# A pooled-attention and mixture-of-experts kernel: values summed by one operation, the first two hidden chunks joined, and a wait on output moved to the next job

## The chip, the core and the metric

The kernel runs on one core of a Trainium2 chip. A core has five engines that run their own instruction streams and meet only at semaphores: TensorE (PE in the profile, with its weight loads as PEld), VectorE (DVE), ScalarE (ACT), GpSimd (POOL) and SyncE (SP, which issues DMAs). The metric is the device time of one execution in microseconds (us), lower is better. Before the change the median of three runs is 604.17 us (603.97 to 604.62).

## The reference, cut to what matters

Attention over 8 batches, 8 heads and 576 positions, with keys and values averaged over groups of 8 neighbours (576 rows become 72), then a mixture of 8 experts of which each token takes one.

```python
k_p = k.reshape(B, H, Sp, pool, D).mean(axis=3)        # pool = 8, Sp = 72, D = 64
v_p = v.reshape(B, H, Sp, pool, D).mean(axis=3)
attn = softmax(scale * q @ k_p.T)                      # 576 x 72
x = (attn @ v_p), heads side by side                   # 4608 tokens x 512
e_idx = argmax(x @ w_gate); gate_w = its softmax share
eom = sigmoid(x @ w_output_gate)
h = relu(x[mask] @ w1[e]);  ye = h @ w2[e]             # 512 -> 1024 -> 512
out[mask] = gate_w * eom * ye
```

## The kernel before, in words

**Attention and routing** (the first 150 us) work on 36 tiles of 128 tokens, each in two halves of heads (a = 0, 1). Per half PE makes scores (L275) into `p_h`, DVE takes the row maximum `m` (L281), ACT the exponentials (L287), PE transposes them (`ptr`, L299), ACT copies them to SBUF, PE multiplies them with the pooled values `vbd` into `p_y` (L309), and DVE takes reciprocals (L326) and writes the normalised rows `xg` (L332). There are two `p_y` banks, one for each half, so the next tile's L309 of a half waits for this tile's L332 of that half.

For each of the batches 1 to 7 the values arrive by DMA in `vt` (a view of the buffer `rows`): 5 chunks of 128 partitions x 512 numbers, which are 8 neighbours x 64. GpSimd adds the upper 256 to the lower 256 of each chunk (`halve_v`, L223: chunks 0 to 2 as part 0, chunks 3 and 4 as part 1). DVE then adds 128 to 128 (in `rows`) and 64 to 64 (into `vp`), for each part, by `pool_v` (L227). GpSimd also sums the keys (`kq`, L201), which ACT scales into `kbd` (L206), and issues the scatters of finished rows to the experts' lists (L440), one for each tile.

The order on each engine is the order of the Python calls. `plan` fixes most steps to a half tile; small DVE steps (the pooling of values, `pooled`, and the routing of four tiles, `route`) stand in a queue, from which `work` takes two units after the row maximum, one after the values' matmuls and one after the normalisation. Each `yield` of `pooled` or `route` ends a unit. `pooled` is put at the queue's head.

**The tail** (152 to 175 us) is written as the string `TAIL`: the first expert's first layer for the first 384 tokens, in eight chunks of 128 hidden units. `M` is the 12 matmuls of a chunk (L659, into one of three `p_h` banks or `p_y1`), `H` the relu on ACT (L516), `L` its low part on DVE (L520), `a`/`d` and `A`/`D` the high and low halves of weights (L468, L472), `W` units of the queue (the routing of the last tiles, and the job table), `R` the first rows' places, `T` each engine's load of the table, `Y` three matmuls of the second layer (L665). Then all engines meet at a barrier (L1393).

**The experts** (175 us on) run jobs of three or two slots of 128 tokens. PE does the first layer (L1015) and the second (L996), DVE scales the result into one of three buffers (L1186), and GpSimd scatters it to `out` (L1328). GpSimd's job is `body` in the block from L1260 on: it waits for the earlier outputs, copies weights and row numbers (L1321, L1322), gathers the ids two jobs ahead (L1305), scatters its slots, and waits until all of its scatters have landed. The kernel ends at a second barrier (L1361).

Of the kernel before, what the change touches and what calls it, by code (L numbers as in the profile page):

```python
# [16 lines left out]
ALU = mybir.AluOpType  # L17
AX = mybir.AxisListType
PSUM = bass.MemoryType.PSUM

B, H, S, D = 8, 8, 576, 64
KEYS, POOL = 72, 8
N, DM, FF, E = B * S, H * D, 1024, 8
P = 128
NT = N // P
WIDE = 3
# [4 lines left out]
R = 56  # L31
# [26 lines left out]

TAIL = 'M W9 a H L W3 d M a H L W6 d M a H L W6 d M a H L W6 d A M H L W12 A D M H L A D R M H L A D T M D Y Y Y Y Y H L'.split()
F0 = TAIL.count('Y')

AHEAD = {3: 8, 2: 8, 1: 2}
# [26 lines left out]
def attention_and_routing(ctx, tc, sh, qT, kT, v, wg, wst, xs):  # L91
    nc = tc.nc
# [11 lines left out]
    vt = sh.rows[:, 0:5 * DM].rearrange("p (c f) -> p c f", c=5)  # L104
# [113 lines left out]
    def part_v(a):  # L218
        return slice(3 * a, 3 + 2 * a)
# [5 lines left out]
    def pool_v(b, a, n):  # L225
        to = vt[:, part_v(a), 0:n] if n > D else pooled_rows(b)[:, part_v(a)]
        nc.vector.tensor_tensor(to, vt[:, part_v(a), 0:n], vt[:, part_v(a), n:2 * n], op=ALU.add)  # L227

    def first_v(a):
        for n in (4 * D, 2 * D, D):  # L230
            pool_v(0, a, n)

    def place_v(b, c):
        t = vbd[b % 2]
# [250 lines left out]
    halves = list(range(AHEAD_OF_X, 8))  # L485
    layered, high, low, outputs, split_piece, split_done = [], [], [], [], [], [3, 2, 1, 0]

    def first_layer(kind):
        if kind == "M":
            f = len(layered)  # L490
            layered.append((sh.p_h + sh.p_y[1:])[f % 4][:, 0:WIDE * P])
            hidden_chunk(nc, sh, f, layered[f], f == 0)
        elif kind == "Y":
            outputs.append(output_chunk(nc, sh, len(outputs), sh.p_y[0], 0))
        elif kind == "a":
            split_hi(halves[0])
        elif kind == "d":
            split_lo(halves.pop(0))
        elif kind == "A":
            split_piece.append(len(split_piece))  # L500
            split_hi(2 * 4 + split_piece[-1], 1)
        elif kind == "D":
            split_lo(2 * 4 + split_done.pop(), 1)
        elif kind == "T":
            assert not queue
            for eng in (nc.tensor, nc.scalar, nc.vector, nc.gpsimd, nc.sync):
                sh.loaded[eng.engine] = nc.values_load_multi_w_load_instructions(
                    sh.table[0:1, 0:E + 2], [eng.engine], min_val=0, max_val=1023,
                    skip_runtime_bounds_check_because="counts of a few bits each")[1]
        elif kind == "R":  # L510
            slot_rows(lambda ins: None, nc.vector, sh, past_rows(sh, 0, 2 * WIDE), line_rows(sh, 0, 2 * WIDE), sh.number[:, 0:2 * WIDE],
                      sh.base[:, :, 0:2 * WIDE], sh.ids[:, 0:2 * WIDE], sh.at[:, 0:2 * WIDE])
        elif kind == "H":
            f = len(high)
            high.append(f)
            nc.scalar.activation(sh.ht[:, 0, f], layered[f], AF.Relu)  # L516
        else:
            f = len(low)
            low.append(f)
            nc.vector.scalar_tensor_tensor(sh.ht[:, 1, f], layered[f], 0.0, sh.ht[:, 0, f].bitcast(F32),  # L520
                                           op0=ALU.max, op1=ALU.subtract)
# [5 lines left out]

    def pooled(b):
        for a in range(2):
            for n in (2 * D, D):  # L530
                pool_v(b, a, n)
                yield 0

    tick = [0]

# [14 lines left out]
    for b in range(1, B):  # L550
        f = S * b // P + 0.5 * (b % 2)
# [77 lines left out]
    for step in sorted(x for x in plan if x > NT + 2):  # L629
        for f, args in plan[step]:  # L630
            f(*args)
    for step in TAIL:
        if step[0] == "W":
# [16 lines left out]
    return x.rearrange("p g f -> p (g f)"), x.rearrange("p g (d t) -> p d g t", d=4), halves  # L650


def hidden_chunk(nc, sh, f, acc, late):
    terms = [(d, part, x) for d in range(4) for part, x in ((0, 0), (0, 1), (1, 0))]
    if late:
        terms.sort(key=lambda term: term[2])
    for d, part, x in terms:
        o = DM * f + P * d
        i = nc.tensor.matmul(acc, sh.w1[0][:, part, o:o + P], sh.xt[:, x, d, :], start=((d, part, x) == terms[0]), stop=((d, part, x) == terms[-1]))  # L659
    return i  # L660


def output_chunk(nc, sh, f, acc, k):
# [64 lines left out]
def experts(st, nc, sh, wst, xs, out):  # L728
# [9 lines left out]
    yb = [y_all[:, DM * k:DM * k + DM] for k in range(WIDE)]  # L738
# [11 lines left out]
    q = {k: st.enter_context(nc.semaphore("m_" + k)) for k in names}  # L750
# [535 lines left out]
    @blk.gpsimd  # L1286
    def _(eng):
        copy = nc.gpsimd.tensor_copy

        def columns(u):  # L1290
            u = nc.s_assert_within(u, 0, R - WIDE, skip_runtime_bounds_check_because="there are at most 50 slots")
            return ids[:, bass.ds(u, WIDE)]

        def past(name, val):
            val = eng.to_reg(val)
            eng.wait_ge(q["on"], 1)
            eng.wait_ge(q[name], val)

        def take(u):
            copy(nx, xm[:, :, ID - DM:ID - DM + 2]).then_inc(q["c"], 1)  # L1300
            copy(src, columns(u)).then_inc(q["c"], 1)  # L1301

        def gather(sems):
            for k in range(WIDE):
                nc.gpsimd.indirect_dma_start(out=xm[:, k].bitcast(I32), out_offset=None, in_=xs,  # L1305
                                             in_offset=bass.IndirectOffsetOnAxis(ap=src[:, k:k + 1], axis=0)).then_inc(sems[k], 16)

        def ahead(u, job, more):
            if not isinstance(job, int):
                for k in range(WIDE):  # L1310
                    past(f"x{k}", 16 * job - 16)
            with eng.If(more > 0):
                take(u + 3)
            with eng.If(more <= 0):
                take(u + 2)
            past("c", 3 * job + 1)
            gather(X)

        def body(e, size, job, u, single, nth, more, last, late):
            past("y", u + 1)  # L1320
            copy(sc[:, 0:3:4 - size], nx[:, 0:size, 1]).then_inc(q["sc"], 1)  # L1321
            copy(dst, nx[:, :, 0]).then_inc(q["c"], 1)  # L1322
            past("sc", job + 1)
            past("c", 3 * job + 5)
            ahead(u + size, job + 2, more)
            for k in range(size):
                past("y", u + k + 2)
                nc.gpsimd.indirect_dma_start(out=out, out_offset=bass.IndirectOffsetOnAxis(ap=dst[:, k:k + 1], axis=0),  # L1328
                                             in_=yb[2 if k == size - 1 else k], in_offset=None, bounds_check=N - 1, oob_is_err=False).then_inc(q["out"], 16)
            past("out", 16 * (u + size))  # L1330

        eng.nop().then_inc(q["on"], 1)
        rows = table(eng)
        with eng.If(rows[E + 1] > 2):
            eng.nop().then_inc(q["c"], 2)
        with eng.If(rows[E + 1] <= 2):
            copy(src, columns(0)).then_inc(q["c"], 2)
            past("c", 2)
            gather([q["g"]] * WIDE)
            past("g", 16 * WIDE)  # L1340
        ahead(0, 1, rows[E + 1] & 1)
        eng.wait_ge(q["t"], ROWS)
        job, slot = loops(eng, rows, body)
        for k in range(WIDE):
            past(f"x{k}", 16 * job + 16)


def program():
# [54 lines left out]
def layout(q, k, v, moe_w_gate, moe_w_output_gate, moe_w1, moe_w2):  # L1403
    c = np.ascontiguousarray
    gates = np.concatenate([moe_w_gate, moe_w_output_gate], axis=1).reshape(H, D, GATE)
    wg = np.zeros((2, D, 11, GATE), np.float32)
    for a, slot, head in ((0, 0, 0), (0, 1, 1), (1, 2, 3), (1, 3, 4), (0, 4, 1), (0, 5, 2), (1, 6, 6), (1, 7, 7), (0, 8, 4), (0, 9, 5), (0, 10, 6)):
        wg[a, :, slot] = gates[head]
    rows = v.reshape(B, H, KEYS, POOL * D)
    vs = np.zeros((B, P, 5, POOL * D), np.float32)  # L1410
    for chunk, r0, head, k0, n in VROWS:
        vs[:, r0:r0 + n, chunk] = rows[:, head, k0:k0 + n]
    return {
        "qT": c(q.reshape(B, 4, 2, S, D).transpose(0, 2, 4, 1, 3)).reshape(B, P, 4 * S),
        "kT": c(k.reshape(B, 4, 2, KEYS, POOL, D).transpose(0, 2, 5, 1, 4, 3)).reshape(B, P, 4 * POOL * KEYS),
        "v": vs.reshape(B, P, 5 * POOL * D),
        "wg": wg.reshape(P, 11 * GATE),
        "wst": c(np.concatenate([
            moe_w1.reshape(E, H, D, FF).transpose(0, 2, 1, 3).reshape(E, 4, 4, 32, FF).transpose(0, 1, 3, 2, 4).reshape(E, P, 4, 8, P).transpose(0, 1, 3, 2, 4).reshape(E, P, 4096),
            moe_w2.reshape(E, 8, P, DM).transpose(0, 2, 1, 3).reshape(E, P, 4096)], axis=2)),  # L1420
    }
# [6 lines left out]
```

## Time and profile before

| | |
|---|---|
| median of three runs | 604.17 us |
| the profiled execution | 603.94 us, of which the span that the profile covers is 602.1 us |
| PE busy | 572.3 us (95%) |
| DVE, ACT, POOL busy | 365.1, 257.8, 223.1 us |
| TensorE's granted clock | full speed in every slice |

Times in the rows count from the start of the span. Where an operation of DVE overlaps the next one by some hundredths, this is its pipeline: a start-to-start distance is then what it costs. "Idle before" is put down to the event that came last.

### The profile page before, as it was taken

What the parts mean: (1) busy time and instruction counts of PE and PEld (TensorE: products, weight loads), DVE (VectorE), ACT (ScalarE), POOL (GpSimd) and SP (SyncE); (2) the same over time, 40 slices, a digit from 0 to 9 for tenths busy, and PEclk for the clock granted to TensorE, in tenths of its full rate; (3) what the DMA queues carried; (4) which work ended last, traced back from release to release, by engine and by line L of the source; (5) the groups of instructions that cost most, each with busy time, mean ns of one, the idle gap of its engine ahead of it and who ended that gap; (6) DMA issues with size and microseconds to landing.
All of it is one profiled execution on the core that took longest, in us unless ns stands there. A gap on an engine that the chain in (4) does not pass through costs nothing.

```text
span 602.1 us, 11826 instructions
## 1 busy us (share of the span) xinstructions
PE 572.3 (95%) x3427; PEld 519.2 (86%) x3428; DVE 365.1 (61%) x892; ACT 257.8 (43%) x709; POOL 223.1 (37%) x331
## 2 busy tenths in 40 slices
PE   2999999999899999999999999999999999999996
PEld 2898898888888989898989898898988898989894
DVE  6789999988888625698575323664263842232323
ACT  2988998787435304266344120441141420302120
POOL 2858789642524322233234131231202421213131
PEclk9999999999999999999999999999999999999999
DMA  9856899966377433589666213463033212010111
GB/s 337 312 236 270 316 349 369 348 232 198 140 238 182 170 99 118 147 234 335 177 215 201 62 37 88 139 195 65 35 139 102 46 21 84 2 52 19 41 30 36
DMA packets 44684, 96.61 MB, mean 160 GB/s; under 512 B 5515, under 2 KB 28475, under 8 KB 41664
## 3 DMA queue, kind: packets, MB, share of 16 engines
q1 hardware_dynamic: 29328, 48.95, 25.3%
q10 hardware_dynamic: 7488, 27.27, 13.5%
q0 software_dynamic: 7792, 19.61, 9.3%
q14 instruction: 57, 0.47, 0.3%
q8 instruction: 19, 0.31, 0.2%
HBM read 76.36 MB, written 22.91 MB: 165 GB/s over the span
## 4 chain that ended last, share of the span: by engine, by line
PE 68%; issue 2%; DVEq 0%; DVE 0%; POOL 0%; POOLq 0%
PE p_h L1015 34%; PE p_y L996 33%; PE p_y L665 1%; POOL out L1328 0%; DVE rows L1186 0%; DVEq L1189 0%; PE p_y L1050 0%; DVE q_even L1212 0%; DVEq L779 0%; DVEq L780 0%; DVEq L1219 0%; DVEq L910 0%; DVEq L837 0%; DVEq L1211 0%; DVEq L860 0%
## 5 line engine op out<-in xcount | busy, mean ns | idle before, releaser
L1095 ACT ACTIVATE ht<-p_h 128x384 fp32r<-128x384 f32 (+1 forms) x104 | 46.9, 451 | 245.9 <-PE p_h L1015 243.7
L1015 PE MATMUL p_h<-xt,w1b 128*128 128x384 f32 (+1 forms) x736 | 115.5, 317 | 1.9 <-issue 1.3
L1015 PEld LDWEIGHTS p_h<-xt,w1b 128*128 128x128 f32 x736 | 114.4, 189 | 3.2 <-issue 2.8
L1328 POOL DMA_INDIRECT out<-rows,dst x41 | 43.1, 1051 | 199.8 <-DVE rows L1186 196.6
L1197 DVE SCALAR_TENSOR_TENSOR ht<-p_h,ht 128x384 fp32r<-128x384 f32 (+1 forms) x104 | 52.3, 504 | 98.4 <-ACT ht L1095 98.3
L996 PE MATMUL p_y<-w2b,ht 128*128 128x512 f32 x480 | 110.4, 390 | 0.0
L996 PEld LDWEIGHTS p_y<-w2b,ht 128*128 128x128 f32 x480 | 89.8, 188 | 18.4
L1015 PE MATMUL p_h<-xt,w1a 128*128 128x256 f32 (+1 forms) x640 | 93.7, 306 | 1.2 <-DVE q_even L1212 1.0
L1015 PEld LDWEIGHTS p_h<-xt,w1a 128*128 128x128 f32 x640 | 92.8, 190 | 2.3 <-DVE q_even L1212 1.2
L996 PE MATMUL p_y<-w2a,ht 128*128 128x512 f32 x408 | 94.2, 390 | 0.4 <-PE p_y L665 0.4
L996 PEld LDWEIGHTS p_y<-w2a,ht 128*128 128x128 f32 x408 | 76.2, 188 | 16.4 <-issue 0.9
L1186 DVE TENSOR_SCALAR rows<-p_y,sc 128x512 f32<-128x512 f32 x41 | 30.1, 741 | 85.9 <-PE p_y L996 71.5
L287 ACT ACTIVATE p<-p_h,m 128x72 f32<-128x72 f32 x288 | 69.9, 345 | 13.4 <-DVE m L281 13.0
L309 PE MATMUL p_y<-vbd,pT 128*128 128x162 f32 (+3 forms) x400 | 68.5, 320 | 3.8 <-DVE xg L332 2.6
L1305 POOL DMA_INDIRECT rows<-xs,src x51 | 56.0, 1099 | 24.9 <-POOL src L1301 13.4
L309 PEld LDWEIGHTS p_y<-vbd,pT 128*128 128x128 f32 (+1 forms) x400 | 54.2, 179 | 8.7 <-issue 2.5
L440 POOL DMA_INDIRECT xs<-xg,where x36 | 36.1, 1003 | 42.5 <-DVE grec L326 20.7
L201 POOL TENSOR_TENSOR kq<-kq 128x288 f32<-128x288 f32 (+1 forms) x63 | 40.8, 673 | 15.0 <-DMA kq<-kT 14.2
L275 PE MATMUL p_h<-kbd,q_even 128*128 128x144 f32 (+1 forms) x160 | 28.9, 308 | 11.6 <-DMA q_even<-qT 8.8
L332 DVE TENSOR_TENSOR xg<-p_y,grec 128x240 f32<-128x240 f32 x72 | 35.3, 490 | 1.3
L1150 DVE STREAM_TRANSPOSE turned<-rows 128x512 f32<-128x512 f32 x51 | 32.4, 686 | 4.0 <-DMA rows<-xs 2.2
L275 PEld LDWEIGHTS p_h<-kbd,q_even 128*128 128x128 f32 (+1 forms) x160 | 22.9, 191 | 13.7 <-issue 9.3
(170 smaller groups left out, 660.3 us busy)
## 6 DMA issues: line engine op xcount, KB each, us to landing
stage<-wst ACTq DMA_DIRECT2D x52, 512.0 KB, 4.7
rows<-v SPq DMA_DIRECT2D x8, 1280.0 KB, 6.3
kq<-kT SPq DMA_DIRECT2D x7, 1152.0 KB, 12.0
rows<-xs SPq DMA_DIRECT2D x36, 192.0 KB, 3.8
stage<-wst SPq DMA_DIRECT2D x12, 512.0 KB, 6.0
kq<-qT SPq DMA_DIRECT2D x4, 1152.0 KB, 9.5
q_even<-qT SPq DMA_DIRECT2D x3, 1152.0 KB, 8.8
rows<-xs SPq DMA_DIRECT2D x20, 128.0 KB
```

The lines of the kernel that those rows point to most:

```text
L201: eng.tensor_tensor(k[:, :, 0:w], k[:, :, 0:w], k[:, :, w:2 * w], op=ALU.add)
L275: nc.tensor.matmul(s[r0:r0 + n, 144 * c:144 * c + 144], q_t[b][:, 2 * a + c, s0:s0 + n], kbd[b % 2][:, 2 * a + c, :], start=True, stop=True)
L287: nc.scalar.activation(pt[i % 3][:, o:o + KEYS], sv[:, h], AF.Exp, bias=m[:, h:h + 1])
L309: nc.tensor.matmul(av[r0:r0 + n, COLS * h:COLS * (h + n_heads)], pT[:, c, r0:r0 + n], vbd[b % 2][:, slot:slot + n_heads].rearrange("p h f ...
L332: nc.vector.tensor_tensor(xg[g][:, j, 0:LEAD + DM].rearrange("p (f h) -> p f h", h=H)[:, :, hs], avv[:, :, 0:GATE + D].rearrange("p h f -> ...
L440: ins = nc.gpsimd.indirect_dma_start(out=whole_rows(xs), out_offset=bass.IndirectOffsetOnAxis(ap=where, axis=0), in_=x.bitcast(I32), in_of ...
L996: i = mm(to, ht[:, h, f, P * k:P * k + P], w[:, part, o:o + DM], start=(f == 0 and part == 0 and h == 0), stop=(f == 7 and h == 1))
L1015: i = mm(to, w[:, part, o:o + P], x, start=(d == 0 and k == 0), stop=(d == 3 and k == len(terms) - 1))
L1095: act(ht[:, 0, f, 0:size * P], p_h[f % DEEP][:, 0:size * P], AF.Relu).then_inc(q["hh"], 1)
L1197: nc.vector.scalar_tensor_tensor(ht[:, 1, f, 0:n], src, 0.0, ht[:, 0, f, 0:n].bitcast(F32), op0=ALU.max, op1=ALU.subtract).then_inc(q["hl" ...
L1305: nc.gpsimd.indirect_dma_start(out=xm[:, k].bitcast(I32), out_offset=None, in_=xs, in_offset=bass.IndirectOffsetOnAxis(ap=src[:, k:k + 1], ...
L1328: nc.gpsimd.indirect_dma_start(out=out, out_offset=bass.IndirectOffsetOnAxis(ap=dst[:, k:k + 1], axis=0), in_=yb[2 if k == size - 1 else k ...
```

## The change

It has three parts.

1. For batches 1 to 7 the two DVE additions of a part become one `tensor_reduce` over four neighbours (`sum_v`). The host lays the values of these batches out so that the four neighbours that are left after GpSimd's addition are adjacent. `pooled` has two units instead of four, so the units of `route` behind it move up.
2. `TAIL` loses its last `M`, and the first `M` makes chunks 0 and 1 together (`hidden_chunks`): first all products with the high part of the tokens, of both chunks, then those with the low part. PE is one chunk further ahead in the rest of the tail.
3. GpSimd's wait for its scatters stands at the start of the next job instead of the end of this one, and after the last job behind the waits for the gathers. The bound of the scatters is kept in a register (`limit`).

```diff
-TAIL = 'M W9 a H L W3 d M a H L W6 d M a H L W6 d M a H L W6 d A M H L W12 A D M H L A D R M H L A D T M D Y Y Y Y Y H L'.split()
+TAIL = 'M W9 a H L W3 d M a H L W6 d M a H L W6 d M a H L W6 d M A H L W12 A D M H L A D R M H L A D T D Y Y Y Y Y H L'.split()
...
+    def sum_v(b, a):
+        nc.vector.tensor_reduce(pooled_rows(b)[:, part_v(a)],
+                                vt[:, part_v(a), 0:POOL // 2 * D].rearrange("p c (d r) -> p c d r", d=D), axis=AX.X, op=ALU.add)
...
         if kind == "M":
-            f = len(layered)
-            layered.append((sh.p_h + sh.p_y[1:])[f % 4][:, 0:WIDE * P])
-            hidden_chunk(nc, sh, f, layered[f], f == 0)
+            accs = {}
+            for _ in range(1 if layered else 2):
+                f = len(layered)
+                accs[f] = (sh.p_h + sh.p_y[1:])[f % 4][:, 0:WIDE * P]
+                layered.append(accs[f])
+            hidden_chunks(nc, sh, accs)
...
     def pooled(b):
         for a in range(2):
-            for n in (2 * D, D):
-                pool_v(b, a, n)
-                yield 0
+            sum_v(b, a)
+            yield 0
...
-def hidden_chunk(nc, sh, f, acc, late):
-    terms = [(d, part, x) for d in range(4) for part, x in ((0, 0), (0, 1), (1, 0))]
-    if late:
-        terms.sort(key=lambda term: term[2])
...
+def hidden_chunks(nc, sh, accs):
+    terms = [(f, d, part, x) for f in accs for d in range(4) for part, x in ((0, 0), (0, 1), (1, 0))]
+    if 0 in accs:
+        terms.sort(key=lambda term: term[3])
...
         def body(e, size, job, u, single, nth, more, last, late):
+            with eng.If(job > 0):
+                past("out", 16 * u)
             past("y", u + 1)
...
-                                             in_=yb[2 if k == size - 1 else k], in_offset=None, bounds_check=N - 1, oob_is_err=False).then_inc(q["out"], 16)
-            past("out", 16 * (u + size))
-
+                                             in_=yb[2 if k == size - 1 else k], in_offset=None, bounds_check=limit, oob_is_err=False).then_inc(q["out"], 16)
+
+        limit = eng.to_reg(N - 1)
...
         for k in range(WIDE):
             past(f"x{k}", 16 * job + 16)
+        past("out", 16 * slot)
...
+    halves = vs[1:].reshape(B - 1, P, 5, 2, POOL // 2, D).transpose(0, 1, 2, 3, 5, 4)
+    vs[1:] = halves.reshape(vs[1:].shape)
```

On DVE, around batch 3's values, these rows stood before (`rows` and `vp` are the values, `m` the row maxima, `grec` and `xg` the normalisation, `gden` and `pos` the routing of tiles 4 to 7):

```order
L281 TENSOR_REDUCE m_1_800<-p_h 128x4
L227 TENSOR_TENSOR rows<-rows 128x3x128
L227 TENSOR_TENSOR vp_803<-rows 128x192
L326 RECIPROCAL grec_721<-p_y 128x5
L227 TENSOR_TENSOR rows<-rows 128x2x128
L332 TENSOR_TENSOR xg_719<-p_y,grec_721 128x80x5
L227 TENSOR_TENSOR vp_803<-rows 128x128
L281 TENSOR_REDUCE m_0_825<-p_h 128x4
L378 TENSOR_REDUCE gden_833<-ex_715 128x4
L382 TENSOR_TENSOR pos_836<-rk_827,running 128x32
```

and these stand now:

```order
L285 TENSOR_REDUCE m_1_796<-p_h 128x4
L234 TENSOR_REDUCE vp_798<-rows 128x192
L234 TENSOR_REDUCE vp_798<-rows 128x128
L330 RECIPROCAL grec_717<-p_y 128x5
L382 TENSOR_REDUCE gden_811<-ex_711 128x4
L336 TENSOR_TENSOR xg_715<-p_y,grec_717 128x80x5
L386 TENSOR_TENSOR pos_819<-rk_805,running 128x32
```

Both sums of values now stand ahead of the reciprocal and of `xg`, where one pair and one half of the other pair stood; routing steps have moved up into the freed places. In the other six batches the sums stand in the same way, with no routing step between the reciprocal and `xg` (in batch 4 two short ones).

On PE, where the tail begins, these rows stood before (L659 are the hidden chunks, L372 and L374 the last tiles' ranks, L665 the second layer; the weight loads between the ranks are left out):

```order
L659 MATMUL p_h<-xt,w1a 128x384 x12
...
L374 MATMUL rk_2312<-oh_2301,ones 128x8
L659 MATMUL p_h<-xt,w1a 128x384 x24
L659 MATMUL p_y<-xt,w1a 128x384 x12
L659 MATMUL p_h<-xt,w1a 128x384 x36
L507 TENSOR_LOAD table
L659 MATMUL p_y<-xt,w1a 128x384 x12
L665 MATMUL p_y<-w2a,ht 128x512 x15
L1393 UNCONDITIONAL_BRANCH
```

and these stand now:

```order
L666 MATMUL p_h<-xt,w1a 128x384 x24
...
L378 MATMUL rk_2310<-oh_2299,ones 128x8
L666 MATMUL p_h<-xt,w1a 128x384 x12
L666 MATMUL p_y<-xt,w1a 128x384 x12
L666 MATMUL p_h<-xt,w1a 128x384 x36
L666 MATMUL p_y<-xt,w1a 128x384 x12
L514 TENSOR_LOAD table
L672 MATMUL p_y<-w2a,ht 128x512 x15
L1403 UNCONDITIONAL_BRANCH
```

Twelve matmuls have moved ahead of the ranks, and the last chunk ahead of the table's load. The orders of ACT and of SP are the same in both kernels.

On GpSimd, at the end of the last job and of the kernel, these rows stood before (L1295 and L780 are arithmetic on registers; waits have no row, and the one for `out` stood between L1295 and L780):

```order
L1328 DMA out<-rows,dst 4608x512
L1295 REGISTER_ALU
L780 REGISTER_ALU
L780 COMPARE_AND_BRANCH
L779 UNCONDITIONAL_BRANCH
L1295 ISA x2
L1361 UNCONDITIONAL_BRANCH
```

and these stand now, with the wait for `out` behind the last register operation:

```order
L1337 DMA out<-rows,dst 4608x512
L787 REGISTER_ALU
L787 COMPARE_AND_BRANCH
L786 UNCONDITIONAL_BRANCH
L1302 ISA x7
L1371 UNCONDITIONAL_BRANCH
```

The loop's end and the register operations stood behind the wait and stand ahead of it; five register operations are new.

## Rows read from the trace of the kernel before

**Rows 1.** Busy time by stretch: PE, PEld, DVE, ACT, POOL, then PEclk, DMA share, GB/s.
```profile
50.00:80.00 30.00, 28.92 (x229) 26.44 (x230) 27.35 (x101) 25.71 (x105) 24.12 (x34) 1.00 0.72 273
152.00:175.00 23.00, 20.85 (x116) 19.24 (x115) 20.27 (x77) 10.14 (x18) 8.23 (x8) 1.00 0.53 186
250.00:602.00 352.00, 344.59 (x1899) 313.88 (x1897) 170.49 (x264) 102.94 (x178) 91.08 (x124) 1.00 0.34 103
```

**Rows 2.** PE's timeline: start us, us, instruction, [idle before, and what ended it].
```profile
26.33 1.20 PE L309 MATMUL p_y<-vbd,pT 128*128 128x162 f32 x6 [0.47 <-DVE xg L332]
...
58.96 1.23 PE L309 MATMUL p_y<-vbd,pT 128*128 128x162 f32 x6 [0.73 <-DVE xg L332]
...
91.91 1.20 PE L309 MATMUL p_y<-vbd,pT 128*128 128x162 f32 x6 [0.30 <-DVE xg L332]
...
127.28 1.20 PE L309 MATMUL p_y<-vbd,pT 128*128 128x162 f32 x6 [0.27 <-DVE xg L332]
...
154.08 0.97 PE L659 MATMUL p_h<-xt,w1a 128*128 128x384 f32 x4 [0.61 <-DVE xt L483]
...
155.82 0.19 PE L372 MATMUL rk<-oh,tri 128*128 128x40 bf16 x1 [0.77 <-DVE oh L363]
...
175.23 0.94 PE L665 MATMUL p_y<-w2a,ht 128*128 128x512 f32 x3 [0.99 <-PEq L1393]
```

**Rows 3.** The chain that ended last, its last step: start us, us, what.
```profile
598.09 1.00 POOL out L1328
```

**Rows 4.** Groups of DVE instructions by shape, 20 to 130 us: busy, mean ns, idle.
```profile
L227 DVE TENSOR_TENSOR rows<-rows 128x384 f32<-128x384 f32 x7 | 6.8, 976 | 1.7 <-POOL rows L223 1.7
L227 DVE TENSOR_TENSOR vp<-rows 128x192 f32<-128x192 f32 x7 | 3.8, 544 | 0.2
L227 DVE TENSOR_TENSOR rows<-rows 128x256 f32<-128x256 f32 x7 | 3.2, 464 | 0.0
L227 DVE TENSOR_TENSOR vp<-rows 128x128 f32<-128x128 f32 x7 | 2.1, 297 | 0.0
```

**Rows 5.** Two lines with sums on DVE: duration ns min/median/max, first and last start, forms.
```profile
L348 DVE TENSOR_REDUCE lg<-xg x9: 671/676/678, 35.9 to 153.9; 128x64 f32<-128x512 f32 x9
...
L687 DVE TENSOR_REDUCE rows<-rows x2: 328/913/1498, 169.8 to 177.8; 128x12 f32<-128x84 f32 x1, 128x100 f32<-128x700 f32 x1
```

**Rows 6.** Timelines of GpSimd, then DVE, batch 3's values, 53 to 62 us.
```profile
53.40 3.77 POOL L223 TENSOR_TENSOR rows<-rows 128x256 f32<-128x256 f32 x5
...
61.38 0.99 POOL L440 DMA_INDIRECT xs<-xg,where  x1 [2.32 <-DVE grec L326]
...
55.53 1.07 DVE L227 TENSOR_TENSOR rows<-rows 128x384 f32<-128x384 f32 x1 [0.23 <-POOL rows L223]
...
58.34 0.57 DVE L332 TENSOR_TENSOR xg<-p_y,grec 128x400 f32<-128x400 f32 x1
```

**Rows 7.** Timelines of DVE, then PE, batch 4's values, 73 to 76 us.
```profile
73.50 0.67 DVE L227 TENSOR_TENSOR rows<-rows 128x384 f32<-128x384 f32 x1
...
74.87 0.40 DVE L332 TENSOR_TENSOR xg<-p_y,grec 128x240 f32<-128x240 f32 x1
...
75.81 0.58 PE L309 MATMUL p_y<-vbd,pT 128*128 128x162 f32 x3
```

**Rows 8.** DVE's timeline in the tail, 157 to 175 us.
```profile
157.41 0.56 DVE L520 SCALAR_TENSOR_TENSOR ht<-p_h,ht 128x384 fp32r<-128x384 f32 x1 [1.14 <-ACT ht L516]
...
173.64 0.55 DVE L520 SCALAR_TENSOR_TENSOR ht<-p_y,ht 128x384 fp32r<-128x384 f32 x1
```

**Rows 9.** Timelines of GpSimd, then DVE, in the experts, 203 to 213 us.
```profile
203.63 0.19 POOL L1321 COPY sc<-nx 128x3 f32<-128x3 f32 x1 [5.41 <-DMA out<-rows,dst]
...
211.47 0.75 DVE L1186 TENSOR_SCALAR rows<-p_y,sc 128x512 f32<-128x512 f32 x1 [0.18 <-PE p_y L996]
```

**Rows 10.** GpSimd's sequencer after 596 us, two lines: duration ns, first and last start.
```profile
L780 POOLq ALU_OP  x1: 35/35/35, 600.9 to 600.9; - x1
...
L1361 POOLq COMPARE_BRANCH  x1: 38/38/38, 601.7 to 601.7; - x1
```

More of the change, by code (lines that the diff above doesn't have):

```diff
@@ L650, in turned_rows @@
     return x.rearrange("p g f -> p (g f)"), x.rearrange("p g (d t) -> p d g t", d=4), halves
-def hidden_chunk(nc, sh, f, acc, late):
-    terms = [(d, part, x) for d in range(4) for part, x in ((0, 0), (0, 1), (1, 0))]
-    if late:
-        terms.sort(key=lambda term: term[2])
-    for d, part, x in terms:
+def hidden_chunks(nc, sh, accs):
+    terms = [(f, d, part, x) for f in accs for d in range(4) for part, x in ((0, 0), (0, 1), (1, 0))]
+    if 0 in accs:
+        terms.sort(key=lambda term: term[3])
+    seen = {f: 0 for f in accs}
+    for f, d, part, x in terms:
         o = DM * f + P * d
-        i = nc.tensor.matmul(acc, sh.w1[0][:, part, o:o + P], sh.xt[:, x, d, :], start=((d, part, x) == terms[0]), stop=((d, part, x) == terms[-1]))
-    return i
+        nc.tensor.matmul(accs[f], sh.w1[0][:, part, o:o + P], sh.xt[:, x, d, :], start=(seen[f] == 0), stop=(seen[f] == 11))
+        seen[f] += 1
 def output_chunk(nc, sh, f, acc, k):
```

## The prediction

> **What bounds the kernel now.** I read the busy time by stretch first. The experts, 352 of the 602 us, are PE's: it is busy 344.59 us there, and DVE, ACT and GpSimd less than half [rows 1]. The change leaves the orders of PE, DVE and ACT in the experts as they are, so only GpSimd's part could matter there. In the attention PE is busy 28.92 of 30 us while DVE has 27.35 [rows 1]: PE sets the pace, and DVE can hold it up only where its queue is behind for a moment. So the second view is PE's timeline with its idle times. Four of the gaps are of one kind: PE's values' matmuls wait for DVE's `xg`, at 26.33, 58.96, 91.91 and 127.28 us [rows 2], each right behind DVE's pooling of the values of an odd batch (1, 3, 5, 7). They are 0.47 + 0.73 + 0.30 + 0.27 = 1.77 us. In the tail PE waits 0.61 us for the low part of the tokens, 0.77 us for the choice of the last tiles' experts, and 0.99 us at the barrier [rows 2]. The third view is the end of the chain that ended last: GpSimd's last scatter, 598.09 to 599.09 us [rows 3], while the span ends at 602.1.
>
> **Part 1, the values.** For each of seven batches four additions go, of 976 + 544 + 464 + 297 = 2281 ns [rows 4]. In come two reduces that read 768 and 512 numbers of each partition. The nearest row is L348, which reads 512 adjacent numbers from SBUF in 671 to 678 ns, all nine times [rows 5]; so part 1 (512) is 0.68 us. The largest rate that a row shows is L687's 1498 ns for 700 numbers, 2.14 ns each [rows 5], but it reads with a stride; 0.68 us over 512 is 1.32 ns each, fixed part included. By the latter part 0 (768) is at most 1.01 us; taking the fixed part as 0.14 us (L348 at 1.05 ns a number, an estimate) it is 0.94, which I use. A batch then has 0.94 + 0.68 = 1.62 us, 0.66 less than now, 4.6 us of DVE over seven batches. By L687's rate it would be 1.64 + 1.10 = 2.74 us, 0.46 more. I take L348, which reads adjacent numbers as the new reduces do.
>
> DVE's time is not PE's. What counts is when `xg` is written. Batch 3: GpSimd's five additions run from 53.40 to 57.17 us, and the first pair on DVE can start at 55.53 [rows 6]. Now the first reduce ends at 55.53 + 0.94 = 56.47, and the second must wait for GpSimd's fifth addition, which is an operand's last write; it ends by 57.17, or about 56.85 if it no longer shares its time with DVE's additions (3.77 / 5 = 0.75 us each on average, with the longest beside DVE). The second reduce ends at 56.85 + 0.68 = 57.53, the reciprocal and a routing step of 0.17 us each follow, and `xg` starts at 57.85 where it started at 58.34 [rows 6]: 0.49 us of the 0.73 go. The bounds are 0.17 (GpSimd not sooner) and 0.73. For the other three odd batches the wait for GpSimd's fifth addition decides in the same way, between nothing and the whole 0.47 + 0.30 + 0.27 = 1.04 us; I take half, 0.52. Together **1.0 us**, between 0.2 and 1.8.
>
> The even batches have no gap, and there the new order puts both reduces ahead of `xg`. In batch 4 the first addition starts at 73.50 and `xg` at 74.87 [rows 7], 1.37 us later. Now it is 0.94 + 0.68 + 0.17 (reciprocal) = 1.79 us: `xg` from 75.29 to 75.69 us, and the matmul that waits for it starts at 75.81 [rows 7]. It fits with 0.12 us to spare, cost nothing; if the cover is gone each tenth more is a tenth for PE, in three batches.
>
> What moves with it: the rank matmuls of one group stand half a tile earlier on PE, and one group's first scatter stands ahead of two key sums on GpSimd. Behind that scatter are the key sums of batch 4, ACT's scaling and PE's scores. GpSimd stood still for 2.32 us ahead of this scatter anyway [rows 6], and the routing steps that make the row numbers have moved up too, so the two sums are done little later or sooner than now. I count nothing, with 0.4 us to lose (an estimate).
>
> **Part 2, the tail.** The joined chunks give PE 16 matmuls instead of 8 before the low part is wanted and 24 before the ranks. Four of them took 0.97 us [rows 2], so 8 or 12 more are longer than the waits of 0.61 and 0.77 us, which should shrink to nearly nothing. What is late next? DVE. It is busy 20.27 of 23 us in the tail [rows 1]; after its 1.14 us wait at 157.41, which is for ACT's relu of chunk 0 behind the exponential of the routing and a weight half, it has no other, and its last operation runs from 173.64 to 174.19 us [rows 8]. PE ends at 175.23 - 0.99 = 174.24 [rows 2]. All engines meet at the barrier behind both. DVE's order in the tail does not change, so PE can come at most 0.05 us earlier to anything: **0.05 us**, between 0 and 1.4 if I misread who ends last.
>
> **Part 3, GpSimd's wait.** In the loop it goes from a job's end to the next job's start, with the same copies behind it. The copy of `sc` at 203.63 is 7.84 us ahead of the DVE operation that needs it at 211.47, and this is the smallest such distance [rows 9]; a branch more or a register move less is nothing beside that. At the end of the kernel it is different. The last scatters have landed when the register operation of L780 starts at 600.9, and then come the loop's end, two register operations and three waits that are long fulfilled, until the branch to the barrier at 601.7 [rows 10]: 0.8 us after the landing in which nothing is awaited. Now this work, and five register operations more (less than as much again, as today's whole end with its two is 0.8 us), stands ahead of the wait, in the 1.8 us between the scatter's end at 599.09 [rows 3] and 600.9. **0.8 us**, between 0.6 and 0.9.
>
> **Sum.** 1.0 + 0.05 + 0.8 = 1.85 us off the profiled execution's 603.94 us (span 602.1, 1.84 around it), 602.09. The median of the runs lies 0.23 us above that execution, so I predict 604.17 - 1.85 = **602.3 us**.
>
> **A rule against the change.** The additions of a batch write 384 + 192 + 256 + 128 = 960 numbers and the reduces read 1280; only the mean of 2281 ns, which holds DVE's time beside GpSimd's additions, makes them dearer [rows 4]. The Trainium skill (VectorE: DVE Perf Modes, Rules for kernel authors) expects one element a cycle of `tensor_reduce`, calls it the slowest operation of the engine and advises to restructure a hot path away from it. By that rule nothing is gained in the attention, which is the first rival below; L348's constant 0.68 us speaks against its being worse than that.
>
> **Rivals.**
> - *Only the end is gained.* The gaps of rows 2 come back because the second reduce, at the head of DVE's queue, waits for GpSimd's last addition as long as the old operations took. For: the second pair was interleaved before, the reduces are not. Against: batch 3's working above. 604.17 - 0.85 = 603.3 us.
> - *The tail gains too.* If the barrier is not DVE's but PE's, 0.61 + 0.77 = 1.38 us come on top: 602.3 - 1.4 = 600.9 us. For: PE is the last by 0.05 us. Against: DVE's last operation at 174.19.
> - *Slower: the reduces run at L687's rate.* With 2.74 us, `xg` of an even batch starts 2.91 us after the first reduce instead of 1.37, 1.54 later; 0.54 us are covered (75.81 against 74.87 + 0.40 [rows 7]), 1.0 is PE's, in three batches 3.0. In batch 3 it starts at 55.53 + 2.74 + 0.34 = 58.61, 0.27 later than now, and so about 1.1 in the four odd ones. 604.17 + 4.1 - 0.85 = 607.4 us. It decides from 1.74 us for the two reduces (1.37 + 0.54 - 0.17). For: L687. Against: L348.
> - *The collisions fall elsewhere.* DVE operations with two SBUF operands take two to three times their time beside GpSimd's sums, as the means of rows 4 include. If DVE's routing meets GpSimd's key sums once more in the new phase, PE loses about what the worst such place costs, 0.73 us [rows 2], at two places 1.5: 603.8 us.
>
> **Chances.** The forecast 0.52 (its own range 601.5 to 602.9), only the end 0.22, the tail too 0.12, collisions 0.09, slower by the reduces 0.05. A measurement of this kernel tells 0.2%, 1.2 us, from no change. Faster by more than that (under 602.96): nearly all of the forecast, 0.51, the tail's 0.12, 0.04 of the first rival's lower side: 0.67. Slower: 0.05. Within: 0.28. The range that leaves out two in ten reaches from the tail's case to the collisions': 600.9 to 603.7 us.
>
> **What would show it.** In the profile after: reduces of about 0.94 and 0.68 us at every start, and PE's gaps behind `xg` near 59 and 127 us smaller than 0.3. The tail's gaps before the low part and the ranks gone, but a wait for DVE ahead of the barrier in their place. GpSimd's branch to the last barrier within 0.15 us of the last landing. The prediction is wrong if a reduce of 768 takes over 1.15 us, if a new gap stands behind an even batch, or if the barrier comes earlier by more than the attention has gained.

## The result: 0.55% slower, and the profile after

The changed kernel takes 607.20 us (median of five runs, 605.94 to 609.01) against 604.17: a ratio of 1.0055, interval 1.0034 to 1.0077. The forecast was 602.3. The profiled execution is the fastest of the five: 605.94 us, span 604.2, against 603.94 and 602.1. I explain these 2.1 us from the two traces first. The medians lie 3.0 us apart; the 0.9 us more have no trace of their own here.

What the prediction said of single operations holds. The reduces, as groups of DVE instructions from 20 to 130 us (columns as in [rows 4]):

```profile
L234 DVE TENSOR_REDUCE vp<-rows 128x192 f32<-128x768 f32 x7 | 6.6, 944 | 1.0 <-POOL rows L223 1.0
L234 DVE TENSOR_REDUCE vp<-rows 128x128 f32<-128x512 f32 x7 | 4.8, 682 | 1.3 <-POOL rows L223 1.3
```

They take 0.94 and 0.68 us on average, as forecast. GpSimd's last scatter and its branch to the last barrier (its timeline, then one line of its sequencer: ns, first and last start), in answer to [rows 3, 10]:

```profile
600.98 1.01 POOL L1337 DMA_INDIRECT out<-rows,dst  x1 [4.32 <-DVE rows L1193]
...
L1371 POOLq COMPARE_BRANCH  x1: 38/38/38, 603.8 to 603.8; - x1
```

From the end of the scatter to the end of the span it is 2.2 us, where they were 3.0: the 0.8 us of part 3 are there. PE's timeline, in answer to [rows 2]:

```profile
26.37 1.20 PE L313 MATMUL p_y<-vbd,pT 128*128 128x162 f32 x6 [0.29 <-DVE xg L336]
...
85.20 0.19 PE L376 MATMUL rk<-oh,tri 128*128 128x40 bf16 x1 [1.37 <-ACT pT L304]
...
153.13 4.44 PE L666 MATMUL p_h<-xt,w1a 128*128 128x384 f32 x24 [0.21 <-ACT xt L485]
...
173.98 0.73 PE L672 MATMUL p_y<-w2a,ht 128*128 128x512 f32 x2 [0.69 <-DVE w2a L476]
176.52 9.38 PE L672 MATMUL p_y<-w2a,ht 128*128 128x512 f32 x33 [1.80 <-PEq L1403]
186.34 5.76 PE L1003 MATMUL p_y<-w2a,ht 128*128 128x512 f32 x24 [0.44 <-PE p_y L672]
```

The waits behind `xg` near 59, 92 and 127 us are gone, and so are the two in the tail. But long ones are new: 1.37 us at 85, and 0.69 and 1.80 us around the barrier, where it was 0.99. And the 33 matmuls behind the barrier take 9.38 us; before, PE's timeline had there:

```profile
175.23 7.76 PE L665 MATMUL p_y<-w2a,ht 128*128 128x512 f32 x33 [0.99 <-PEq L1393]
183.43 5.76 PE L996 MATMUL p_y<-w2a,ht 128*128 128x512 f32 x24 [0.44 <-PE p_y L665]
```

PE of the changed kernel by the microsecond (stretch, its length, PE busy, granted clock, DMA share, GB/s) shows why:

```profile
85.00:86.00 1.00, 0.80 (x7) 0.62 1.04 424
86.00:87.00 1.00, 1.00 (x4) 0.50 1.06 442
87.00:88.00 1.00, 1.00 (x6) 0.50 1.00 420
...
175.00:176.00 1.00, 0.00 (x0) 1.00 0.00 0
176.00:177.00 1.00, 0.48 (x2) 1.00 0.00 0
177.00:178.00 1.00, 1.00 (x4) 0.70 0.69 106
178.00:179.00 1.00, 1.00 (x4) 0.50 0.81 328
179.00:180.00 1.00, 1.00 (x4) 0.50 1.04 422
```

The granted clock is 0.50 (1.2 of 2.4 GHz) for some 3 us behind each of the two idle times, and the 33 matmuls that fall into the second take 1.62 us longer. In the kernel before it is full from 17 us to the last matmul. The Trainium skill (TensorE: Matmul & The Clock Gate, What's actually happening) lists the lower level as that of an idle array; the trace agrees that there are these two levels.

Where the first idle time comes from can be seen in the timeline of all engines around 82 to 85 us:

```profile
82.38 1.69 DVE L370 TENSOR_TENSOR zs<-lg,oh 128x32 f32<-128x32 f32 x1
82.46 0.94 POOL L201 TENSOR_TENSOR kq<-kq 128x144 f32<-128x144 f32 x2
...
83.52 1.80 POOL L201 TENSOR_TENSOR kq<-kq 128x144 f32<-128x144 f32 x3
...
84.47 0.17 DVE L372 TENSOR_REDUCE zr<-zs 128x4 f32<-128x32 f32 x1
84.56 0.44 DVE L285 TENSOR_REDUCE m<-p_h 128x4 f32<-128x288 f32 x1
84.68 0.20 ACT L373 ACTIVATE ez<-zr 128x4 f32<-128x4 f32 x1 [1.00 <-DVE zr L372]
84.79 0.36 ACT L304 ACTIVATE pT<-ptr 128x256 f32<-128x256 f32 x1
```

DVE's `zs`, 0.15 to 0.2 us at its shortest, takes 1.69 beside GpSimd's key sums. Behind it in DVE's queue stand `zr` and a row maximum; in ACT's, `ez` waits for `zr` with the copy of `pT` behind it, and PE waits for that. What it costs is seen in the same operations of both kernels, of before:

```profile
82.68 0.65 DVE L366 TENSOR_TENSOR zs<-lg,oh 128x32 f32<-128x32 f32 x1
83.25 0.57 DVE L332 TENSOR_TENSOR xg<-p_y,grec 128x400 f32<-128x400 f32 x1
...
87.74 0.41 DVE L332 TENSOR_TENSOR xg<-p_y,grec 128x240 f32<-128x240 f32 x1
...
110.18 1.70 DVE L354 TENSOR_TENSOR d<-lg,mx 128x32 f32<-128x32 f32 x1
```

and of after, with the `xg` of batch 3 ahead:

```profile
57.60 0.58 DVE L336 TENSOR_TENSOR xg<-p_y,grec 128x400 f32<-128x400 f32 x1
...
83.99 0.57 DVE L336 TENSOR_TENSOR xg<-p_y,grec 128x400 f32<-128x400 f32 x1
...
89.68 0.41 DVE L336 TENSOR_TENSOR xg<-p_y,grec 128x240 f32<-128x240 f32 x1
...
97.09 1.94 DVE L358 TENSOR_TENSOR d<-lg,mx 128x32 f32<-128x32 f32 x1
```

The changed kernel is 0.74 us ahead at batch 3 (58.34 before [rows 6]), 0.74 behind at 84 and 1.94 behind at 89.7: 2.7 us are lost up to there. It isn't the only place. By the same comparison of `xg`, 1.2 us come back at batch 5's values; 2.4 more are lost by 99, where `d` takes 1.94 us (0.62 before); 1.3 come back by 114, where the `d` of the kernel before takes its 1.70 and this one's 0.35. At the end of the attention the changed kernel is 1.35 behind. PE leaves the barrier 1.29 us late (176.52 against 175.23) and starts the next line 2.91 late (186.34 against 183.43), so 1.62 are the clock behind the barrier; with 0.8 gained at the end it is 2.1.

### The profile page after: what moved, and what is told of

It is laid out like the page before. It is cut to its first block, busy times and chain, and to the rows that moved or that the text cites. A ratio compares the mean times of both kernels' runs of the same rounds, so it can differ in the third digit from the quotient of the medians.

```text
span 604.2 us, 11853 instructions
## 1 busy us (share of the span) xinstructions
PE 575.7 (95%) x3427; PEld 522.1 (86%) x3428; DVE 362.9 (60%) x878; ACT 257.4 (43%) x709; POOL 219.0 (36%) x331
## 4 chain that ended last, share of the span: by engine, by line
PE 66%; issue 2%; DVE 1%; DVEq 1%; ACT 0%; POOL 0%; POOLq 0%
PE p_h L1022 33%; PE p_y L1003 32%; PE p_y L672 2%; ACT w2b L1091 0%; DVE q_even L1219 0%; POOL out L1337 0%; DVE rows L1193 0%; DVE ht L1204 0%; DVE xt L1153 0%; DVEq L1196 0%; DVEq L1152 0%; ACT ht L1110 0%; DVEq L786 0%; DVEq L787 0%; DVE w2b L1181 0%
## 5 line engine op out<-in xcount | busy, mean ns | idle before, releaser
L1337 POOL DMA_INDIRECT out<-rows,dst x41 | 41.6, 1014 | 213.4 <-DVE rows L1193 210.9
L285 DVE TENSOR_REDUCE m<-p_h 128x4 f32<-128x288 f32 x72 | 32.4, 450 | 4.3 <-PE p_h L279 3.6
```

## The experiments

A ratio is to the kernel before, run on the same chip at the same time; its median there was 605.5 to 607.9 us. Each kernel had 6 or 12 runs, and one of them was profiled.

**The three parts apart.** Each is the kernel before with one part's hunks of the diff.

> Part 1 alone (the sums of values and their layout; tail and GpSimd's waits as before). Theory A (the loss is TensorE's clock, which falls to its lower level behind an idle time of PE of more than a microsecond; one such idle time comes from DVE's `zs` taking 1.69 us instead of 0.65 beside GpSimd's key sums near 82 us, a place that part 1 makes by its new order): the profile shows the same fall near 85 us, the attention ends about 1.3 us later than before, and the time is about 605.5 us (604.17 + 1.3). Rival B (the attention's gain is as forecast and the fall near 85 us is chance that comes and goes): 603.2 us in most runs, with a spread of more than 2 us. Rival C (the loss needs all parts together): 603.2 us in all runs.

> Part 2 alone (first two chunks joined, the last M of the tail gone). Theory A (PE is done earlier in the tail while DVE, which sets the barrier, is not; PE's idle time of 0.6 and 0.8 us is collected ahead of the barrier, where it stands still for 1.8 us with only two matmuls in the microseconds ahead of it, and the clock is at the lower level for some 3.4 us behind it): the barrier comes at the same time as before or 0.05 us sooner, granted clock 0.5 in the 3 us behind it, and the time is about 604.17 + 1.6 = 605.8 us. Rival C (the barrier's fall of the clock needs the shifted attention): 604.1 us with the clock full behind the barrier.

> Part 3 alone (GpSimd's waits for its scatters). Both theories: the end of the kernel is 0.8 us shorter, nothing else moves, 603.4 us. Rival D (the loss of 3 us comes from GpSimd's new order in the jobs): 604 us or more.

> The changed kernel once more, for a second profile of it. Theory A: clock falls near 85 us and behind the barrier in this profile too; 606 to 609 us. Rival B: at least one of the two is missing, or another one stands elsewhere; that would be what makes its times differ by 3 us from run to run where those of the kernel before differ by 1.3.

| kernel | median us | ratio | interval |
|---|---|---|---|
| part 1 | 606.49 | 1.0016 | 0.9996 to 1.0036 |
| part 2 | 606.37 | 1.0031 | 1.0002 to 1.0059 |
| part 3 | 603.79 | 0.9977 | 0.9956 to 0.9997 |
| all, again | 607.12 | 1.0027 | 1.0003 to 1.0051 |

The parts add up: +0.16 + 0.31 - 0.23 = +0.24%, against +0.27% for all, each within about 0.2 to 0.3%. So no part needs the others (rival C falls), and GpSimd's order in the jobs is a gain (rival D falls). Part 1 alone doesn't show the gain that was forecast, and its loss isn't clear of noise. In it `zs` is 1.69 us again at 82.69, with 1.35 us of idle PE and a clock of 0.5 behind it; part 2 alone shows the fall behind the barrier. In the kernels with the old order (part 2, part 3, and before) `zs` of that group takes 0.65 to 0.66 us. But the second profile of the changed kernel isn't like the first. PE by the microsecond:

```profile
84.00:85.00 1.00, 0.00 (x0) 1.00 1.05 430
85.00:86.00 1.00, 0.81 (x9) 1.00 1.02 418
86.00:87.00 1.00, 1.00 (x10) 1.00 1.04 437
...
117.00:118.00 1.00, 0.77 (x5) 0.79 1.05 444
118.00:119.00 1.00, 1.00 (x9) 0.50 0.85 350
```

The idle time near 85 us is there (1.34 us) and the clock stays full; it falls at 117 instead, behind another idle time of 1.64 us. DVE then GpSimd of part 1 alone show what such a later place is:

```profile
113.61 3.07 DVE L358 TENSOR_TENSOR d<-lg,mx 128x32 f32<-128x32 f32 x1
```

```profile
113.76 4.18 POOL L201 TENSOR_TENSOR kq<-kq 128x288 f32<-128x288 f32 x7
```

The place at 82 us belongs to part 1's order: `zs` takes 1.68 or 1.69 us there in all five profiles with the new order and 0.19 to 0.66 in the ten with the old one (the runs below included, but for the one with `lg` in PSUM). The places from 96 us on differ from run to run, with the old attention too (part 2 alone has `zs` at 2.16 us at 98, the kernel before 0.71 from the same code up to there). Yet the new order has its share there as well: `d` or `cand` takes 1.87 to 1.98 us at 96 to 97 in all five of its profiles and at most 0.75 in the ten others, four of which have an `oh` or a `zs` of 1.46 to 2.16 there. Rival B is thus at most half right; that such places make the spread of the times is plausible, but with a profile or two of each kernel it isn't shown.

**Part 1 with the old order.**

```diff
             sum_v(b, a)
             yield 0
+            yield 0
```

The second `yield` is an empty unit. It keeps the units of `route` behind it in their old places, and with them the scatters on GpSimd.

> Part 1 alone, but each sum of values followed by an empty unit, so that every routing step and every scatter keeps its old place in the orders of DVE and GpSimd. Theory A1 (the loss of part 1 comes from where the moved routing steps meet GpSimd's key sums: `zs` at 82.4 us in all three profiles of kernels with part 1, in none of the three without): `zs` of that group is back at 0.6 to 0.8 us, PE has no gap of 1.35 us near 85 us and keeps the clock there, and the time is 604.17 - 1.0 = 603.2 us, as the prediction had it. Rival A2 (DVE's sums being done sooner shift the phase against GpSimd all the same): a collision of over 1.5 us stands near 82 us or in another group than before, time 605 us or more.

605.58 us, ratio 0.9947 (0.9916 to 0.9978), about 3 us faster where 1.0 was expected. `zs` there takes 0.65 us again and PE has no idle time of 0.2 us or more between 27 and 95 us. The profiled execution is the slowest of the twelve, 609.05 us: in it the clock falls at 101, 248 and 470 us. The decisive pair ran on one chip, parts 1 and 3 with the new and with the old order:

> The changed kernel without part 2 (parts 1 and 3, routing steps moved up as in the change). Theory: the clock stays full behind the barrier, `zs` near 82.5 us takes 1.7 us again and PE stands still for 1.35 us near 85 us. Against the kernel before: +1.0 (part 1 as measured) - 1.0 (part 3), no difference within 0.2%.

> As the run beside it, but with the empty units that keep the routing steps and the scatters in their old places. Theory A1 (the moved order is the loss of part 1): 2 to 4 us below the run beside it, and 0.4% or more below the kernel before. Rival A2 (the order makes no difference, collisions only fall elsewhere): the same time as the run beside it within 1 us.

606.00 us (1.0009, 0.9991 to 1.0026) with the new order, **600.69 us (0.9928, 0.9904 to 0.9952)** with the old. The lines of `zs` (ns min/median/max over nine groups) and GpSimd's timeline, new order first:

```profile
L370 DVE TENSOR_TENSOR zs<-lg,oh x9: 151/193/1691, 39.1 to 158.7; 128x32 f32<-128x32 f32 x9
...
82.83 0.93 POOL L201 TENSOR_TENSOR kq<-kq 128x144 f32<-128x144 f32 x2
83.72 0.20 POOL L325 IOTA xg<- 128x64 f32 x1
83.89 1.79 POOL L201 TENSOR_TENSOR kq<-kq 128x144 f32<-128x144 f32 x3
```

```profile
L370 DVE TENSOR_TENSOR zs<-lg,oh x9: 191/403/806, 38.6 to 153.4; 128x32 f32<-128x32 f32 x9
...
81.29 0.95 POOL L201 TENSOR_TENSOR kq<-kq 128x144 f32<-128x144 f32 x2
82.18 0.21 POOL L325 IOTA xg<- 128x64 f32 x1
82.56 0.99 POOL L444 DMA_INDIRECT xs<-xg,where  x1 [0.17 <-issue]
83.58 1.82 POOL L201 TENSOR_TENSOR kq<-kq 128x144 f32<-128x144 f32 x3
```

With the old order a scatter stands between the two runs of sums; with the new one it has been issued earlier, and five sums follow each other but for an iota (GpSimd's writing of numbers). The order of DVE's operations from 77 us to behind `zs` is the same in both; what differs is that the row numbers (`where`) of the scatters are written one half tile sooner. A1 holds, A2 falls: the sums of values gain, and the new order loses 5.3 us of median, more than the 2 to 4 expected. In the two profiles 5.3 us lie between the ends of the attention, too: about 1.8 of them come from the place at 82 us and 2.6 from behind 96 us. And the version with the old order beats the kernel before, and by its ratio the changed one.

How the scatter's absence holds `zs` up isn't shown. In the kernel before `zs` is done at 83.33, behind the first of the sums, and GpSimd's timeline has the scatter only then:

```profile
84.03 0.99 POOL L440 DMA_INDIRECT xs<-xg,where  x1 [0.17 <-issue]
```

**What holds DVE up.** `lg`, `d` and `cand` into a piece of PSUM that `p_y` leaves free:

```diff
...
-        lg = small(g, [P, n, 16], F32, "lg")
+        spare = sh.p_y[0][:, 256:256 + 32 * n].rearrange("p (c n e) -> p c n e", c=4, n=n)
+        lg = sh.p_y[0][:, 256:256 + 16 * n].rearrange("p (n e) -> p n e", n=n)
...
```

> Part 1 alone, with the routing's `lg`, `d` and `cand` in an unused piece of a PSUM bank instead of SBUF, so that `d`, `cand`, `oh` and `zs` have one operand in SBUF instead of two. Theory A3 (these short operations are held off by GpSimd's sums only while they have two operands in SBUF: `xg`, which reads PSUM and SBUF, is never longer than 0.58 us): no one of the four is longer than 0.4 us, no gap of PE over 0.8 us is left between 20 and 130 us but that at 133 us, the clock is full through the attention, and the time is 604.17 - 1.0 (part 1) - 1.0 (the collisions that the kernel before has near 110 and 113 us) = 602.2 us with a smaller spread. Rival A4 (any operation of DVE is held off by GpSimd): the long ones stay, 605 to 607 us.

`d` over nine groups, and one line of PE's timeline:

```profile
L359 DVE TENSOR_TENSOR p_y<-p_y,mx x9: 199/199/200, 38.6 to 167.1; 128x32 f32<-128x32 f32 x9
...
69.43 0.79 PE L313 MATMUL p_y<-vbd,pT 128*128 128x162 f32 x4 [1.47 <-DVE mx L357]
```

A3's mechanism holds: none of the four (`d`, `cand`, `oh`, `zs`) is over 0.2 us in any group, also where GpSimd's sums run all the while. Its time doesn't: 620.58 us (1.0215, 1.0171 to 1.0259). PE now waits 1.1 to 3.0 us at eight of the nine groups, seven times for DVE's reads of the bank that it writes, and the clock falls behind three idle times (at 37, 119 and 204 us). The rule behind it is in the Trainium skill (SBUF — State Buffer, Who interferes with whom): an operation of DVE with two inputs in SBUF and one of GpSimd that reads SBUF exclude each other, and the second waits for the first. The traces agree on which operations are hit, but "the first" is several: the `d` of 3.07 us in part 1 alone waits through five sums that follow each other.

On GpSimd, parts 1 and 3 with the old order:

```diff
         k = k_t[b][:, c0:c1]
+        if eng is nc.gpsimd:
+            eng.memset(apart, 0.0)
```

> Parts 1 and 3 with the old order, and ahead of each of GpSimd's key sums a memset of one column that reads nothing. Theory G (a short operation of DVE with two operands in SBUF gets no turn as long as GpSimd's sums follow each other within some hundredths of a microsecond, and gets one in any break): none of `d`, `cand`, `oh`, `zs` is longer than 1.0 us, and the time is about 1 us below the run with the old order, with less spread. Rival H (a break of a tenth of a microsecond isn't enough, as one iota of 0.2 us at 83.4 us in the changed kernel was not): operations of 1.5 to 3 us stay, and the time is the same or higher, as GpSimd has 0.1 us more for each sum.

603.73 us (0.9976, 0.9959 to 0.9994), so 3 us more than without the memsets (0.10 us each). DVE's timeline:

```profile
109.80 2.65 DVE L361 TENSOR_TENSOR d<-lg,mx 128x32 f32<-128x32 f32 x1
```

Rival H holds: with memsets of 0.1 us between the sums this `d` still waits for three of them.

**What the clock costs at the barrier.**

```diff
+    def spare():
+        for _ in range(3):
+            nc.tensor.matmul(sh.p_h[0], sh.ht[:, 0, 0, 0:P], sh.w2[0][:, 0, 0:DM], start=True, stop=True)
```

called ahead of the second matmul of the tail's last `Y`, and again behind its third.

> The changed kernel with six matmuls whose result nobody reads in PE's idle time ahead of the barrier: three where it waits 0.69 us for the low part of the second layer's weights, three behind the last matmul. Theory A (the loss behind the barrier is the clock, which falls because PE stood still for 1.8 us with only two matmuls in the microseconds ahead): PE's wait at the barrier is about 1.0 us again, the granted clock behind it is 1.0, the stretch from the barrier to the second layer's next line takes 8.2 instead of 9.8 us, and the time is 1.6 us below the changed kernel's. Rival E (what is slow behind the barrier is the weights' or rows' arrival, since PE comes with less of its second layer done): the stretch still takes 9.8 us with the clock at full.

606.51 us, ratio 0.9977 (0.9947 to 1.0006) where the changed kernel had 1.0027 at another time; behind the barrier the clock is full and the 33 matmuls take 7.74 us. Then part 2 alone, with the six matmuls and without, on one chip:

> Part 2 alone with the six matmuls that nobody reads ahead of the barrier. Theory A: the clock is full behind the barrier and the time is that of the kernel before (DVE sets the barrier, PE's lead is worth nothing): ratio 1.000, and 1.6 us less than the run beside it. Rival F: the lead is worth over 0.5 us: ratio under 0.999. Rival I (the matmuls themselves hold something up): over 1.001 with a full clock.

> Part 2 alone, as in the second run. Theory A: ratio about 1.0027 (1.6 of 604 us), clock at the lower level behind the barrier.

PE's timeline with the matmuls, then without:

```profile
176.66 7.76 PE L678 MATMUL p_y<-w2a,ht 128*128 128x512 f32 x33 [1.12 <-PEq L1406]
184.85 5.76 PE L1009 MATMUL p_y<-w2a,ht 128*128 128x512 f32 x24 [0.44 <-PE p_y L678]
```

```profile
175.38 9.38 PE L669 MATMUL p_y<-w2a,ht 128*128 128x512 f32 x33 [1.95 <-PEq L1397]
185.19 5.76 PE L1000 MATMUL p_y<-w2a,ht 128*128 128x512 f32 x24 [0.44 <-PE p_y L669]
```

603.86 us (0.9964, 0.9935 to 0.9994) against 606.58 (1.0013, 0.9988 to 1.0037). The same 33 matmuls take 7.76 us at the full clock and 9.38 at the lower: 1.62 us, bought back by work that nobody reads. Rival E falls. The time with the matmuls is even below the kernel before, by F's mark (under 0.999) and not A's. But in the profile the tail isn't shorter (24.82 us from the values' last matmuls at 151.84 to the barrier's end, 24.85 before), so where that comes from is open.

The joined chunks with a late last one:

```diff
-TAIL = 'M W9 a H L W3 d M a ...
+TAIL = 'M W9 a H L W3 d a ...
```

> Part 2 alone, with the first two chunks joined but the last one left behind the table's load: the chunk that is missing is the second, so PE is a chunk ahead only up to there. Theory A: PE's waits of 0.61 and 0.77 us in the tail go and come back elsewhere in the tail, the barrier stands at the time of before within 0.1 us (DVE sets it), PE's wait there is 0.99 us and the clock behind it full, so the time is that of before, 604.2 us. Rival F (joining the chunks itself brings the clock down, or PE's lead is worth something once the clock is kept): 605.8 or 602.8 us.

The last `M` stays behind `T`. 610.09 us (1.0029, 1.0000 to 1.0059), and the barrier's wait is 1.82 us with a clock of 0.5 behind it. I had expected 0.99. Theory A falls in this point, and F holds in its first form, that joining the chunks itself brings the clock down: what PE doesn't wait for early in the tail any more, it waits for at the barrier.

The changed kernel with the empty units and the six matmuls:

> The changed kernel with both mendings: the empty units, and six matmuls that nobody reads ahead of the barrier. Theory A: part 2 then costs and gives nothing, since DVE sets the barrier: the time of the run without part 2 and with the old order, within 0.5 us. Rival F (PE's lead in the tail is worth something once the clock stays up): over 0.5 us less than that run.

602.26 us (0.9947, 0.9927 to 0.9968), 1.6 above the version without part 2, with overlapping intervals. Its profile has a full clock behind the barrier, but a place of the other kind, on DVE:

```profile
108.50 4.28 DVE L358 TENSOR_TENSOR d<-lg,mx 128x32 f32<-128x32 f32 x1
```

The same operation took 1.58 us in the profile without part 2, from the same code up to there. So these two runs don't tell whether part 2 is worth anything once mended.

## Why the prediction was wrong

- **Right:** the durations of the reduces, the 0.8 us at the end, and that the gaps behind `xg` go. Batch 3 gained 0.74 us where 0.49 was worked out, and it was lost afterwards. With the old order the attention's gain stayed and was more than forecast: its last `xg` starts at 149.90 us, 2.35 ahead of the kernel before, against 1.0 (0.2 to 1.8). The rival of reduces at L687's rate fell with the first profile; that its 607.4 us lies near the measured 607.2 is chance.
- **Wrong, the largest step:** "What moves with it" was counted at nothing, with 0.4 us to lose. It looked at one group's first scatter and asked only whether the key sums come later, not what a change of GpSimd's order does to DVE's operations beside them. The moved order cost 5.3 us between the two kernels that differ in it alone, and 2.7 us had been lost at 89.7 us in the first profile. The rival "The collisions fall elsewhere" had the mechanism, at 0.09 of the chance, but priced a place at 0.73 us, the attention's worst gap in [rows 2]. The trace of the kernel before already had a `d` of 1.70 us, and an idle time of PE like the 1.37 us at 85 can take the clock with it (not always, see the last section); then the matmuls of the next 3 us pay.
- **Wrong, the tail:** the prediction said that DVE sets the barrier and that PE's waits return ahead of it, a gain of 0.05 us, between 0 and 1.4. The barrier's end came as it said (24.80 us behind the start of the values' last matmuls, 24.85 before), but the part loses 1.62 us: PE's waits of 0.61 and 0.77 us are gathered in the one at the barrier, 1.80 us instead of 0.99, the clock falls behind it, and the sum had no term for the clock.
- **The range** ended at 603.7, because its upper end was two collisions' waits of 0.73 us, without the clock.
- **Against the rule on reduces:** the runs bear out L348's row, 0.68 us; with the old order two reduces instead of four additions are a gain, which the prediction's rule against the change would not have.

## What to carry to other kernels

Where TensorE sets the pace, look at each of its idle times together with the granted clock behind it: an idle time that is gathered from small ones can cost more than they did, and some unread matmuls can be cheaper than the wait. Moving short steps is not free even where the queue has room: look up on VectorE and on GpSimd what then runs side by side, also for operations that keep their place, and hold the old order with empty units if only the operations were to change.

## What the runs showed of the hardware that was not expected

- The clock fell behind idle times of 1.33 to 1.37 us near 85 us in three profiles (the changed kernel, part 1 alone, parts 1 and 3), but not behind those of 1.34 and 1.36 at the same place in two others, nor behind 1.63 us at 117 in part 1 alone or 1.89 us at 253 in part 2 alone. Behind the barrier it fell after 1.80 to 1.95 us each time and never after 0.98 to 1.12. In part 1 with the old order it fell at 101 us behind idle times of 0.79 and 0.63 us. No length by itself decides it in these runs. Nor is the low stretch always some 3 us: that one lasted nearly 7, as in three other profiles.
- A short DVE operation that is held up ends some 0.05 us behind the end of one of GpSimd's sums: `zs` at 82.38 + 1.69 = 84.07, the third sum at 83.52 + 0.48 = 84.00. In these cases it waits for whole sums. Why it gets its turn after one (0.65 us in the kernel before, from the same distance to the first sum) or after many (4.28) is open.
